# Splitting the first load of each batch, sharing the first products between two engines, and moving the softmax inside a pass

## The chip, the cores and the metric

The kernel runs on one core of one Trainium2 chip. The metric is device time in microseconds (us) for one execution. Ratios are computed as the mean time of one kernel's fast runs over that of the other's of the same rounds, so they are not quite the ratio of the medians quoted beside them. Different calls ran on different chips, and the kernel before took 1084 to 1090 us on them; differences of a few microseconds are therefore read from ratios, or from kernels of one call.

## The reference

Eight batches of 4096 tokens with 192 features. Each token gets a weighted sum of itself and the six tokens before it, with weights from a softmax over 7 per head; then two matrix products with `h - tanh(h)` between them.

```python
w = softmax(weight_gen, axis=-1)                  # [8, 4096, 8 heads, 7]
x_pad = concatenate([zeros(8, 6, 192), x], axis=1)
x = einsum('bshk,bskhg->bshg', w, windows_of_7(x_pad))   # -> [32768, 192]
h = x @ w_in                                      # [192, 2048]
out = (h - tanh(h)) @ w_out                       # [2048, 192]
```

## The kernel before

The work is cut into 32 passes of 1024 tokens, four to a batch. A pass `n` has eight steps, counted from 0. In each step TensorE makes two blocks of the first product for `n` (`gemm1`) and one block of the second for `n - 1` (`gemm2`); in steps 2 and 5 it also transposes and sums the seven weighted products for `n + 1` (`conv`). GpSimd makes those products (`products`), two passes ahead, and the softmax runs three passes ahead. The first tile of a batch has no tokens before its first row, so row 0 is loaded apart and its six missing tokens are cleared (`memzero`).

```python
    def load(n):
        ...
        lo = 0
        if s == 0:                                   # first pass of a batch
            lo = 1
            nc.vector.memzero(x_t[0:1, 0:HALO, :])
            nc.sync.dma_start(out=x_t[0:1, HALO : HALO + J, :], in_=x[b, 0:J]...)
        ...
        nc.sync.dma_start(out=x_t[lo:P, :, :], in_=src)     # 127 or 128 partitions

    def softmax(n):
        ...   # exp on ScalarE -> e_t; then on VectorE: zsum, zr = 1/zsum, wsm = e_t*zr

    def products(n):
        for k in range(K):
            nc.gpsimd.tensor_mul(prod_k, x_t[:, k : k + J, :]..., wsm[:, :, :, k : k + 1]...)
    ...
    for n in range(NTOT + 1):
        if n + 2 < NTOT:
            products(n + 2)
        if n + 3 < NTOT:
            load(n + 3)
        for p in range(J):
            ...  # gemm1 twice, gemm2; conv in steps 2 and 5
            if p == 5 and n + 3 < NTOT:
                softmax(n + 3)
```

The x tiles, the products and the output tiles have two buffers each. The blocks of the first product have three in PSUM.

The softmax here doesn't subtract the row's maximum and nothing guards it: scores larger than these inputs give would overflow.

Of the kernel before, what the change touches and what calls it, by code (L numbers as in the profile page):

```python
# [16 lines left out]
def kernel(  # L17
# [8 lines left out]
    nc = tc.nc  # L26

    B, S, D = x.shape
# [3 lines left out]
    P = nc.NUM_PARTITIONS  # L32
    R = P // 2
    HALO = K - 1

    J = 8
# [4 lines left out]
    NTOT = B * NSB  # L41
# [19 lines left out]

    x_of = {}
    wg_of = {}
    wsm_of = {}
    prods_of = {}
    conv_of = {}
# [3 lines left out]
    def load(n):  # L70
        b, s = divmod(n, NSB)
        s0 = s * TOK
        wg_t = wgpool.tile([P, J, H, K], FP32, name="wg_t")
        nc.sync.dma_start(
            out=wg_t[:],
            in_=weight_gen[b, s0 : s0 + TOK].rearrange("(p j) h k -> p j h k", p=P),
        )

        x_t = xpool.tile([P, HALO + J, D], FP32, name="x_t")
        lo = 0  # L80
        if s == 0:
            lo = 1
            nc.vector.memzero(x_t[0:1, 0:HALO, :])  # L83
            nc.sync.dma_start(out=x_t[0:1, HALO : HALO + J, :], in_=x[b, 0:J].rearrange("(p j) d -> p j d", p=1))
        win = x[b, s0 + lo * J - HALO : s0 + lo * J - HALO + 1]
        src = bass.AP(
            tensor=win.tensor,
            offset=win.offset,
            ap=[[J * D, P - lo], [D, HALO + J], [1, D]],
        )  # L90
        nc.sync.dma_start(out=x_t[lo:P, :, :], in_=src)
        wg_of[n] = wg_t
        x_of[n] = x_t

    def softmax(n):
        wg_t = wg_of.pop(n)
        e_t = wgpool.tile([P, J, H, K], FP32, name="e_t")
        nc.scalar.activation(  # L98
            out=e_t[:].rearrange("p j h k -> p (j h k)"),
            in_=wg_t[:].rearrange("p j h k -> p (j h k)"),  # L100
            func=ACT.Exp,
        )
        zsum = wgpool.tile([P, J * H], FP32, name="zsum")
        nc.vector.reduce_sum(  # L104
            out=zsum[:], in_=e_t[:].rearrange("p j h k -> p (j h) k"), axis=AX.X
        )
        zr = wgpool.tile([P, J * H], FP32, name="zr")
        nc.vector.reciprocal(zr[:], zsum[:])  # L108
        wsm = wgpool.tile([P, J, H, K], FP32, name="wsm")
        nc.vector.tensor_mul(  # L110
            wsm[:].rearrange("p j h k -> p (j h) k"),
            e_t[:].rearrange("p j h k -> p (j h) k"),
            zr[:].rearrange("p (n o) -> p n o", o=1).to_broadcast([P, J * H, K]),
        )
        wsm_of[n] = wsm

    def products(n):
        x_t = x_of.pop(n)
        wsm = wsm_of.pop(n)
        prods = []  # L120
        for k in range(K):

            prod = ppool.tile([P, NC, J, H, GC], BF16, name=f"prod{k}", tag=f"prod{k}")
            nc.gpsimd.tensor_mul(  # L124
                prod[:].rearrange("p c j h g -> p j h c g"),
                x_t[:, k : k + J, :].rearrange("p j (h c g) -> p j h c g", h=H, c=NC),
                wsm[:, :, :, k : k + 1]
                .rearrange("p j h (k o) -> p j h k o", o=1)
                .to_broadcast([P, J, H, NC, GC]),
            )  # L130
            prods.append(prod)
        prods_of[n] = prods

    def conv(n, chunks):

        prods = prods_of[n]
        if n not in conv_of:
            conv_of[n] = cpool.tile([P, NC, HT], BF16, name="convT")
        convT = conv_of[n]
        nch = len(chunks)  # L140
        pc = psum_h.tile([P, 2, HT], FP32, name="pc", tag="ph")
        for k in range(K):
            for ci, c in enumerate(chunks):
                for j in range(JH):
                    col = (ci * JH + j) * R
                    for r in range(2):
                        nc.tensor.matmul(  # L147
                            pc[:, r, col : col + R],
                            lhsT=prods[k][r * R : (r + 1) * R, c, 2 * j : 2 * j + 2].rearrange(
                                "p j h g -> p (j h g)"  # L150
                            ),
                            rhs=ident[r * R : (r + 1) * R, r * R : (r + 1) * R],
                            start=(k == 0 and ci == 0 and j == 0),
                            stop=(k == K - 1 and ci == nch - 1 and j == JH - 1),
                        )
        c0 = chunks[0]
        nc.scalar.activation(  # L157
            out=convT[:, c0 : c0 + nch, :].rearrange("p c (j r t) -> p r (c j) t", r=2, t=R),
            in_=pc[:, :, 0 : nch * JH * R].rearrange("p r (cj t) -> p r cj t", t=R),
            func=ACT.Copy,  # L160
        )
        if c0 + nch == NC:
            prods_of.pop(n)

    def gemm1(n, f):
        convT = conv_of[n]
        ph = psum_h.tile([P, 2, HT], FP32, name="ph", tag="ph")
        for c in range(NC):
            for r in range(2):
                nc.tensor.matmul(  # L170
                    ph[:, r, :],
                    lhsT=w_in[r * R : (r + 1) * R, c, f * P : (f + 1) * P],
                    rhs=convT[r * R : (r + 1) * R, c, :],
                    start=(c == 0),
                    stop=(c == NC - 1),
                )
        th = tpool.tile([P, TOK], FP32, name="th")
        ph_f = ph[:].rearrange("p r t -> p (r t)")
        last_act[0] = nc.scalar.activation(out=th[:], in_=ph_f, func=ACT.Tanh)  # L179
        gt = gpool.tile([P, TOK], BF16, name=f"gt{f}", tag=f"gt{f}")  # L180
        nc.vector.tensor_sub(gt[:], ph_f, th[:])  # L181
        g_of.setdefault(n, []).append(gt)
# [4 lines left out]
    def gemm2(i):  # L187
# [30 lines left out]
        if i > 0:  # L218
# [7 lines left out]
            if j == J - 1:  # L226
# [5 lines left out]
                )  # L232

    load(0)

    w_in = const.tile([P, NC, F], BF16, name="w_in")
    for r in range(2):
        for h in range(H):
            nc.gpsimd.dma_start(  # L239
                out=w_in[r * R + h * GC : r * R + (h + 1) * GC],  # L240
                in_=moe_w_in[h * G : (h + 1) * G].rearrange("(c g) f -> g c f", c=NC),
# [3 lines left out]

    ctx.enter_context(tc.manual_schedule())

    softmax(0)
    load(1)
    products(0)  # L250
    softmax(1)
    load(2)
    conv(0, (0, 1))
    conv(0, (2,))
    products(1)
    softmax(2)
    for n in range(NTOT + 1):
        if n + 2 < NTOT:
            products(n + 2)
# [3 lines that stand above are left out]
            if n < NTOT:  # L263
                gemm1(n, 2 * p)
                gemm1(n, 2 * p + 1)
            if n >= 1:
                gemm2((n - 1) * J + p)
            if n + 1 < NTOT:
                if p == 2:
                    conv(n + 1, (0, 1))  # L270
                if p == 5:
                    conv(n + 1, (2,))
            if p == 5 and n + 3 < NTOT:
                softmax(n + 3)
    gemm2(NTOT * J)


# [28 lines left out]
```

## Time and profile before

| | kernel before |
|---|---|
| median time | 1084.96 us (1082.41 to 1086.94, 4 runs) |
| span of the profiled run | 1082.9 us |
| busy: TensorE, VectorE, ScalarE, GpSimd | 74%, 62%, 59%, 60% |
| GpSimd waiting for x | 267.6 us in 8 waits |
| pass, undisturbed | 24.74 us |
| stop per batch | 23.2 us (worked out in the prediction; 23.6 once a misread start is corrected, see "Why the prediction was right") |

A line of a wait view reads: who waited, for what, total us, times, longest us. A timeline line reads: start, length, engine, line and operation, count, and in brackets how long the engine had been idle and what released it. The distance from one GpSimd set of seven products to the next is the length of a pass, a handy ruler. The lines themselves are in the prediction.

### The profile page before, as it was taken

Reading aid. Unit: us, or ns where it says so; the run is one execution under the profiler, and the core shown is the slowest. Engines: PE = TensorE matmul, PEld = TensorE weight load, DVE = VectorE, ACT = ScalarE, POOL = GpSimd, SP = SyncE. Lnnn points to the kernel's source line nnn. Section 1 sums busy time; section 2 is a strip of 40 time slices with the busy share of each in tenths; the row PEclk is TensorE's granted clock in tenths of the full one; section 3 lists DMA queues with packets and bytes.
Section 4 is the critical chain, followed back from the end, with each engine's and each line's share of the span. In section 5 each row is a group of like instructions: output and inputs, shape, how many; then the busy total and the mean of one; then the engine's idle time right before and its main releaser. Section 6 shows DMA issues by size and latency. Waiting matters only on the chain.

```text
span 1082.9 us, 36083 instructions
## 1 busy us (share of the span) xinstructions
PE 801.6 (74%) x16640; PEld 614.9 (57%) x16640; DVE 676.3 (62%) x616; ACT 642.6 (59%) x865; POOL 655.0 (60%) x247
## 2 busy tenths in 40 slices
PE   0004598689659993899749993899849993999996
PEld 0002276567446772777537772677637772777775
DVE  1003575588538882788628883788728883788782
ACT  0002465577437872687637882688627882787882
POOL 3029970999068771978259770978359770988200
PEclk9999799799869997999969997899969997999999
DMA  4501113141303222230402212130402212130001
GB/s 70 121 24 61 60 36 110 44 144 47 116 19 113 73 86 88 78 107 19 144 20 94 90 64 108 60 113 32 145 21 91 93 65 108 73 107 31 32 32 60
DMA packets 16952, 81.19 MB, mean 75 GB/s; under 512 B 4128, under 2 KB 8224, under 8 KB 12712
## 3 DMA queue, kind: packets, MB, share of 16 engines
q1 hardware_dynamic: 13712, 76.51, 19.7%
q0 software_dynamic: 3088, 2.36, 1.8%
q8 instruction: 130, 2.13, 0.8%
q14 instruction: 22, 0.18, 0.1%
HBM read 56.06 MB, written 25.17 MB: 75 GB/s over the span
## 4 chain that ended last, share of the span: by engine, by line
PE 47%; DMA 22%; DVE 10%; another core or an unknown queue 3%; issue 2%; ACT 2%; POOL 1%; DVEq 0%; ACTq 0%
PE po L200 22%; DMA out_dram<-out_sb 22%; PE ph L170 19%; PE pc L147 6%; DVE gt L181 5%; DVE wsm L110 3%; DVE zsum L104 1%; POOL prod L124 1%; ACT e_t L98 1%; DVE zr L108 1%; ACT out_sb L225 0%; ACT th L179 0%; ACT convT L157 0%; DVEq L110 0%
## 5 line engine op out<-in xcount | busy, mean ns | idle before, releaser
L124 POOL TENSOR_TENSOR prod<-x_t,wsm 128x1536 bf16<-128x1536 f32 x224 | 643.7, 2910 | 332.3 <-DMA x_t<-in_x_dram 267.6
L181 DVE TENSOR_TENSOR gt<-ph,th 128x1024 bf16<-128x1024 f32 x512 | 599.1, 1217 | 262.9 <-ACT th L179 259.9
L179 ACT ACTIVATE th<-ph 128x1024 f32<-128x1024 f32 x512 | 500.6, 1022 | 94.6 <-PE ph L170 93.6
L200 PE MATMUL po<-w_out,gt 64*128 64x192 bf16 x8192 | 398.5, 247 | 119.9 <-ACT out_sb L225 118.9
L200 PEld LDWEIGHTS <-gt 64*128 64x128 bf16 x8192 | 366.0, 96 | 175.5 <-issue 124.1
L170 PE MATMUL ph<-convT,w_in 64*128 64x512 bf16 x3072 | 404.6, 383 | 55.0 <-DVE gt L181 51.0
L170 PEld LDWEIGHTS <-w_in 64*128 64x128 bf16 x3072 | 167.4, 95 | 183.0 <-issue 92.9
L225 ACT ACTIVATE out_sb<-po 128x192 f32<-128x192 f32 x256 | 85.2, 333 | 166.4 <-DMA out_dram<-out_sb 120.6
L147 PE MATMUL pc<-ident,prod 64*128 64x64 bf16 x5376 | 99.5, 195 | 101.8 <-POOL prod L124 100.4
L147 PEld LDWEIGHTS <-prod 64*128 64x128 bf16 x5376 | 95.1, 98 | 104.7 <-POOL prod L124 102.0
L157 ACT ACTIVATE convT<-pc 128x1024 bf16<-128x1024 f32 x64 | 51.8, 810 | 91.2 <-PE pc L147 91.2
L104 DVE TENSOR_REDUCE zsum<-e_t 128x64 f32<-128x448 f32 x32 | 19.8, 620 | 116.5 <-ACT e_t L98 116.5
L98 ACT ACTIVATE e_t<-wg_t 128x448 f32<-128x448 f32 x32 | 18.2, 568 | 83.2 <-DMA wg_t<-in_weight_gen_dram 83.2
L110 DVE TENSOR_TENSOR wsm<-e_t,zr 128x448 f32<-128x448 f32 x32 | 34.4, 1076 | 2.7
L239 POOL DMA_DIRECT2D w_in<-in_moe_w_in_dram x16 | 9.4, 592 | 19.6 <-DMA w_in<-in_moe_w_in_dram 19.2
L108 DVE RECIPROCAL zr<-zsum 128x64 f32<-128x64 f32 x32 | 17.7, 553 | 1.1
L83 DVE MEMSET x_t<- 1x1152 uint32 x8 | 8.1, 1018 | 3.0 <-issue 1.1
L244 POOL DMA_DIRECT2D w_out<-in_moe_w_out_dram x1 | 1.2, 1203 | 1.9 <-DMA w_in<-in_moe_w_in_dram 1.9
L98 ACT ACT_TABLE_LOAD x1 | 1.3, 1283 | 0.7 <-PEq L290 0.7
masks.py:197 POOL MEMSET ident<- 128x128 bf16 x1 | 0.2, 205 | 0.3 <-POOLq L290 0.3
masks.py:199 POOL TENSOR_SCALAR_AFFINE_SELECT ident<-ident 128x128 bf16<-128x128 bf16 x1 | 0.3, 304 | 0.1
L290 POOL MEMSET const-float32-0.0<- 128x1 f32 x1 | 0.1, 98 | 0.2 <-issue 0.2
(3 smaller groups left out, 0.3 us busy)
## 6 DMA issues: line engine op xcount, KB each, us to landing
x_t<-in_x_dram SPq DMA_DIRECT2D x24, 1344.0 KB
out_dram<-out_sb SPq DMA_DIRECT2D x32, 768.0 KB
x_t<-in_x_dram SPq DMA_DIRECT2D x8, 1333.5 KB
wg_t<-in_weight_gen_dram SPq DMA_DIRECT2D x32, 224.0 KB
w_in<-in_moe_w_in_dram POOLq DMA_DIRECT2D x16, 96.0 KB, 19.0
w_out<-in_moe_w_out_dram POOLq DMA_DIRECT2D x1, 768.0 KB, 49.1
x_t<-in_x_dram SPq DMA_DIRECT2D x8, 6.0 KB
```

The lines of the kernel that those rows point to most:

```text
L98: nc.scalar.activation(out=e_t[:].rearrange("p j h k -> p (j h k)"), in_=wg_t[:].rearrange("p j h k -> p (j h k)"), func=ACT.Exp,)
L104: nc.vector.reduce_sum(out=zsum[:], in_=e_t[:].rearrange("p j h k -> p (j h) k"), axis=AX.X)
L108: nc.vector.reciprocal(zr[:], zsum[:])
L110: nc.vector.tensor_mul(wsm[:].rearrange("p j h k -> p (j h) k"), e_t[:].rearrange("p j h k -> p (j h) k"), zr[:].rearrange("p (n o) -> p n ...
L124: nc.gpsimd.tensor_mul(prod[:].rearrange("p c j h g -> p j h c g"), x_t[:, k : k + J, :].rearrange("p j (h c g) -> p j h c g", h=H, c=NC), ...
L147: nc.tensor.matmul(pc[:, r, col : col + R], lhsT=prods[k][r * R : (r + 1) * R, c, 2 * j : 2 * j + 2].rearrange("p j h g -> p (j h g)"), rh ...
L157: nc.scalar.activation(out=convT[:, c0 : c0 + nch, :].rearrange("p c (j r t) -> p r (c j) t", r=2, t=R), in_=pc[:, :, 0 : nch * JH * R].re ...
L170: nc.tensor.matmul(ph[:, r, :], lhsT=w_in[r * R : (r + 1) * R, c, f * P : (f + 1) * P], rhs=convT[r * R : (r + 1) * R, c, :], start=(c == ...
L179: last_act[0] = nc.scalar.activation(out=th[:], in_=ph_f, func=ACT.Tanh)
L181: nc.vector.tensor_sub(gt[:], ph_f, th[:])
L200: mm = nc.tensor.matmul(po[:, 0:D], lhsT=g_of[n][f][r * R : (r + 1) * R, col : col + P], rhs=w_out[r * R : (r + 1) * R, f, :], start=(r == ...
L225: last_act[0] = nc.scalar.activation(out=out_sb[:, j, :], in_=po[:, 0:D], func=ACT.Copy)
```

## The change

Its intent: speed up the first load of a batch, which takes 55 us for 1333.5 KB, shorten the way to the first matrix product, and take the softmax out of the way of TensorE.

```diff
@@ load
+        def rows(p0, p1):
+            ...                      # one x load of partitions p0 to p1
         if s == 0:
-            lo = 1
             nc.vector.memzero(x_t[0:1, 0:HALO, :])
             ...                      # row 0
+            rows(1, 16)
+            rows(16, P)
+        else:
+            rows(0, P)
@@ softmax -> softmax_exp (ScalarE) and softmax_norm (VectorE)
@@ products
+            eng = nc.vector if k in on_vector else nc.gpsimd
+            eng.tensor_mul(
@@ before the loop
-    products(0)
+    products(0, on_vector=(1, 3, 5, 6))
...
-    products(1)
+    products(1, on_vector=(2, 5))
@@ in the loop
+            if p == 1 and n + 3 < NTOT:
+                softmax_exp(n + 3)
             if n >= 1:
                 gemm2((n - 1) * J + p)
...
-            if p == 5 and n + 3 < NTOT:
-                softmax(n + 3)
+            if p == 2 and n + 3 < NTOT:
+                softmax_norm(n + 3)
```

More of the change, by code (lines that the diff above doesn't have):

```diff
@@ L63 @@
     wg_of = {}
+    e_of = {}
     wsm_of = {}
@@ L79, in load, with softmax_exp @@
         x_t = xpool.tile([P, HALO + J, D], FP32, name="x_t")
-        lo = 0
+        def rows(p0, p1):
+            win = x[b, s0 + p0 * J - HALO : s0 + p0 * J - HALO + 1]
+            nc.sync.dma_start(
+                out=x_t[p0:p1, :, :],
+                in_=bass.AP(
+                    tensor=win.tensor,
+                    offset=win.offset,
+                    ap=[[J * D, p1 - p0], [D, HALO + J], [1, D]],
+                ),
+            )
         if s == 0:
-            lo = 1
             nc.vector.memzero(x_t[0:1, 0:HALO, :])
-            nc.sync.dma_start(out=x_t[0:1, HALO : HALO + J, :], in_=x[b, 0:J].rearrange("(p j) d -> p j d", p=1))
-        win = x[b, s0 + lo * J - HALO : s0 + lo * J - HALO + 1]
-        src = bass.AP(
-            tensor=win.tensor,
-            offset=win.offset,
-            ap=[[J * D, P - lo], [D, HALO + J], [1, D]],
-        )
-        nc.sync.dma_start(out=x_t[lo:P, :, :], in_=src)
+            nc.sync.dma_start(
+                out=x_t[0:1, HALO : HALO + J, :],
+                in_=x[b, 0:J].rearrange("(p j) d -> p j d", p=1),
+            )
+            rows(1, 16)
+            rows(16, P)
+        else:
+            rows(0, P)
         wg_of[n] = wg_t
         x_of[n] = x_t
-    def softmax(n):
+    def softmax_exp(n):
         wg_t = wg_of.pop(n)
@@ L102, in softmax, with softmax_norm @@
         )
+        e_of[n] = e_t
+    def softmax_norm(n):
+        e_t = e_of.pop(n)
         zsum = wgpool.tile([P, J * H], FP32, name="zsum")
@@ L115, in softmax, with products @@
         wsm_of[n] = wsm
-    def products(n):
+    def products(n, on_vector=()):
         x_t = x_of.pop(n)
@@ L123, in products @@
             prod = ppool.tile([P, NC, J, H, GC], BF16, name=f"prod{k}", tag=f"prod{k}")
-            nc.gpsimd.tensor_mul(
+            eng = nc.vector if k in on_vector else nc.gpsimd
+            eng.tensor_mul(
                 prod[:].rearrange("p c j h g -> p j h c g"),
@@ L246 @@
     ctx.enter_context(tc.manual_schedule())
-    softmax(0)
+    softmax_exp(0)
+    softmax_norm(0)
     load(1)
-    products(0)
-    softmax(1)
+    products(0, on_vector=(1, 3, 5, 6))
+    softmax_exp(1)
+    softmax_norm(1)
     load(2)
@@ L254 @@
     conv(0, (2,))
-    products(1)
-    softmax(2)
+    products(1, on_vector=(2, 5))
+    softmax_exp(2)
+    softmax_norm(2)
     for n in range(NTOT + 1):
```

## The prediction

> **What bounds the kernel now.** I read the page's busy shares first, then the waits by total, then the chain of work that ended last between 360 and 460 us, then the timelines of the SyncE queue, TensorE, GpSimd and VectorE around one of its long pieces.
>
> Busy shares and waits:
>
> ```profile
> PE 801.6 (74%) x16640; PEld 614.9 (57%) x16640; DVE 676.3 (62%) x616; ACT 642.6 (59%) x865; POOL 655.0 (60%) x247
> ...
> POOL prod L124 <- DMA x_t<-in_x_dram: 267.6, 8, 41.2
> ...
> ACT out_sb L225 <- DMA out_dram<-out_sb: 120.6, 6, 23.5
> PE po L200 <- ACT out_sb L225: 118.9, 15, 22.6
> ```
>
> No engine is above 74%: something stops all of them together. GpSimd waits 8 times for x, once for each of the 8 batches (a batch is four passes of 1024 tokens). ScalarE waits 6 times for an output store to finish, and TensorE then waits for ScalarE. The queue and the chain show one of these (start, length):
>
> ```profile
> 374.05 0.25 SPq L91 DMA_DIRECT2D x_t<-in_x_dram  x1
> 384.62 11.77 SPq L229 DMA_DIRECT2D out_dram<-out_sb  x1
> ...
> 384.62 46.36 DMA out_dram<-out_sb
> ...
> 431.45 2.74 PE L200 MATMUL po<-w_out,gt 64*128 64x192 bf16 x32 [18.20 <-ACT out_sb L225]
> ...
> 429.27 20.06 POOL L124 TENSOR_TENSOR prod<-x_t,wsm 128x1536 bf16<-128x1536 f32 x7 [30.80 <-DMA x_t<-in_x_dram]
> ```
>
> The batch's first x load leaves at 374.05 and GpSimd can start on it at 429.27: 55 us for 1333.5 KB, some 25 GB/s. The store that left after it lands at 431, although a store is only 768 KB. TensorE stops for 18.2 us, and its next 32 matmuls take 2.74 us instead of the usual 1.32 us.
>
> Between such stops the kernel is bound by TensorE. GpSimd starts a set of seven products every 24.74 us (599.08 to 623.82, and 843.56 to 868.29), and in one such stretch (columns: PE, PEld, DVE, ACT, POOL busy, then granted clock, DMA share, GB/s):
>
> ```profile
> 843.50:868.30 24.80, 23.96 (x524) 18.55 (x521) 20.52 (x20) 20.06 (x28) 20.07 (x8) 1.00 0.16 52
> ```
>
> TensorE is busy for 23.96 of 24.80 us at full clock. The largest hole in it is 0.75 us, behind the softmax:
>
> ```profile
> 869.35 0.82 PE L170 MATMUL ph<-convT,w_in 64*128 64x512 bf16 x6 [0.75 <-DVE gt L181]
> ```
>
> [...] wsm takes 0.62 us when GpSimd is idle and up to 3.33 us beside the products, while the reduction, with one input, stays at 0.62 us.
>
> **The change, part by part.**
>
> Split load, at the 7 later batches. 1 + 15 + 112 partitions: [...] What each stop costs is read from where passes start. Pass 1 begins its first matmuls at about 132.8 us and pass 31 at 1037.4: 904.6 us for 30 passes. Thirty undisturbed ones take 30 x 24.74 = 742.2, so 162.4 us, or 23.2 per batch, is the stops. I expect all of it to go.
>
> Start. Now GpSimd begins its products at 74.64, because the first x load takes from 1.55 to there. [...] So after the change I estimate x in place at 8 to 10 us, GpSimd free of its DMA issue at 17 (33.4 now), and w_in there at 25 to 28. VectorE makes products 1, 3, 5 and 6: 1536 elements by the rate of wsm (448 elements in 0.62 us, about 0.15 of it fixed) is 1.75 us each, 7 us, done before GpSimd starts. GpSimd's three take 3 x 2.87 = 8.6: at 25 to 26. The first set thus ends near 26 instead of 95. [...] The third, 20.06 us on GpSimd alone: 63. Pass 0 is short (no second matmul) and ends near 58, but pass 1 needs the third set, also because VectorE's clearing of the x tile of batch 1 waits for it. So pass 1 starts effectively at 62 instead of 132.8: 71 us gained. Of this the load is most; the shared products are worth about 10 us, by 20.06 - 8.6 in the first set and 2 in the second.
>
> Softmax apart. The same instructions run: one exp (0.57) and 0.62 + 0.55 + 0.62 on VectorE. Exp goes to step 1 of 8 of a pass and the normalisation to step 2, beside 1.63 us of transposing matmuls that need no VectorE, where it stood at step 5 beside 0.83. VectorE also saves its 0.47 us wait for exp. By itself that would close most of the 0.75 us hole. But now the products start right after wsm, so wsm always meets an idle GpSimd in undisturbed passes. With the normalisation early they will start once step 5 has freed their buffers, and run about 20 us, to some 13 us into the next pass. Step 2's wsm, some 9 us in, falls among them and waits up to 2.87 us. The place is nearly fixed: from the end of step 5 to wsm is about 16.5 to 17 us, and a product boundary lies at 6 x 2.87 = 17.2. So I expect a wait near 0.5 us, with 2.9 possible if it just misses. A pass without any hole would take 24.74 - 0.75 = 24.0; I take 24.4.
>
> Sum: 62 + 30 x 24.4 + 2 (seven clearings, about 0.3 each) + the last 45.5 (1037.4 to 1082.9, unchanged) = 841.5. Launch times lie a microsecond above the span: 842 us.
>
> **The rivals.** (a) *The normalisation collides with the products.* With a full 2.87 us wait in each pass, a pass takes up to 26.5 and the kernel 905. For it: the 3.33 us wsm now. Against: three PSUM buffers and the 1.63 us of transposes absorb part, and the geometry favours a short wait. (b) *Start bound by the weights.* If the w_in loads keep their pace of 2.3 us whatever x does, GpSimd is free at 33.4, w_in lands at 50, pass 1 starts near 76: 856. [...] (c) *The store wait remains*, [...]: at half of today's stops, 81 us more, 923. Against: with 128-partition loads now the queue issues in 0.33 us and no store wait appears. (d) *TensorE throttled when it no longer rests.* Against: granted clock 1.00 throughout 930 to 1080 us. [...]
>
> **Range and chances.** Pass length 24.0 to 25.2 gives 830 to 866 with the start at 62; a start of 55 to 76 moves it by -7 to +14. These partly offset: 822 to 868. Every part of the big sum would have to fail for a gain under 2% (22 us), as the start alone is worth 71: faster 0.985, same 0.01, slower 0.005.
>
> **What would show it.** Right: no wait of the products for x beyond the start; the store waits under 5 us in all; the first product before 20 us, on VectorE at about 1.75 us; pass 1 starting near 62; sets of products 24.0 to 25 us apart; granted clock near 1.00 after the start. Wrong: passes above 25.5 us with wsm near 3 us (rival a); GpSimd's first product after 30 us (rival b); a long store at batch starts (rival c). My weakest number is the pass length, since every 0.1 us in it is 3 us of the total.

The sum came to 841.5 us, 842 with the launch. The start was built like this: GpSimd free of its issue at 17 us, its three products to 26, the second set of 17.9 us to 43, the third of 20.06 us to 63, and from these pass 1 effectively at 62. The 8 to 10, the 17 and the 25 to 28 us there rested on estimates; so did the time in which the split load should land, 3.4 us. What the trace of the kernel before shows of its long load: from 416 to 427 us, while it and one output store were under way, the mean busy share of the core's 16 DMA engines was 0.06, at 26 GB/s.

## The result, and the profile after

The changed kernel takes 861.48 us (median of 4 runs, 859.23 to 864.49), a ratio of 0.7943 to the kernel before, 95% interval 0.7911 to 0.7975.

The page of the changed kernel, its span and its busy line:

```profile
span 860.7 us, 36095 instructions
...
PE 779.2 (91%) x16640; PEld 604.4 (70%) x16640; DVE 707.5 (82%) x622; ACT 641.3 (75%) x865; POOL 644.9 (75%) x241
```

TensorE now works for 91% of the time. The engines have no less to do (GpSimd handed six products to VectorE, some 10 us on either): the time came out of standing still. Waits by total, changed kernel:

```profile
POOL prod L141 <- PE pc L164: 121.7, 28, 8.3
...
ACT out_sb L242 <- PE po L217: 36.2, 73, 1.9
...
DVE prod L141 <- DMA x_t<-in_x_dram: 9.5, 2, 8.5
...
PE po L217 <- ACT out_sb L242: 3.8, 9, 0.4
```

GpSimd no longer waits for x at all; it waits for TensorE to free product buffers, as an engine with time to spare should. ScalarE's wait for output stores is gone, and TensorE's wait for ScalarE fell from 118.9 us to 3.8. The two large pieces of the split load, from the page's list of transfers (KB each, then median us from issue to landing):

```profile
x_t<-in_x_dram SPq DMA_DIRECT2D x8, 1176.0 KB, 7.0
...
x_t<-in_x_dram SPq DMA_DIRECT2D x8, 157.5 KB, 3.2
```

7.0 us in place of some 55. While the pieces of one such load were under way, with logits beside them (72.6 to 79.7 us), the mean busy share of the 16 DMA engines was 0.85, at 220 GB/s, against the 0.06 and 26 GB/s of the long load. Now two stretches of the changed kernel, an ordinary pass and one in which a batch's first tile is cleared (columns as in the prediction: length, then busy us of PE, PEld, DVE, ACT, POOL, clock, DMA share, GB/s):

```profile
120.50:144.30 23.80, 23.69 (x532) 18.53 (x524) 20.83 (x20) 19.88 (x28) 20.45 (x7) 1.00 0.29 102
...
467.00:494.00 27.00, 24.34 (x554) 18.76 (x548) 24.07 (x22) 20.43 (x28) 20.19 (x8) 1.00 0.38 125
```

In the ordinary one TensorE is idle for 0.11 us of 23.80. In the other it is idle for 2.66. The ruler, GpSimd's timeline of the changed kernel, shows both kinds:

```profile
144.33 20.45 POOL L141 TENSOR_TENSOR prod<-x_t,wsm 128x1536 bf16<-128x1536 f32 x7 [3.38 <-PE pc L164]
168.16 20.06 POOL L141 TENSOR_TENSOR prod<-x_t,wsm 128x1536 bf16<-128x1536 f32 x7 [3.38 <-PE pc L164]
196.56 20.45 POOL L141 TENSOR_TENSOR prod<-x_t,wsm 128x1536 bf16<-128x1536 f32 x7 [8.34 <-PE pc L164]
```

23.83 us, then 28.40. Six such long distances stand in the trace: 28.40, 28.33, 26.75, 26.74, 26.74 and 28.40. What happens in one of them, on VectorE and TensorE, below the normalisation of an ordinary pass (436.11):

```profile
436.11 1.04 DVE L126 TENSOR_TENSOR wsm<-e_t,zr 128x448 f32<-128x448 f32 x1
...
474.88 1.02 DVE L94 MEMSET x_t<- 1x1152 uint32 x1 [0.18 <-PE po L217]
...
484.42 3.25 DVE L126 TENSOR_TENSOR wsm<-e_t,zr 128x448 f32<-128x448 f32 x1
...
488.86 0.82 PE L187 MATMUL ph<-convT,w_in 64*128 64x512 bf16 x6 [2.04 <-DVE gt L198]
```

The clearing makes VectorE late, wsm takes 3.25 us instead of 1.04, the subtraction behind it is late, and TensorE stands for 2.04 us. The products' rhythm shows how narrow the miss is: in that pass a product began at 484.29 us, 0.13 us before wsm was due, and wsm ended 0.48 us after that product's end at 487.19; in the ordinary pass it was due 0.56 us before a product's end (436.67), and ended 0.48 us after it too. The first of the seven later clearings (76.87 us) meets no collision: wsm takes 0.83 us there.

In three of the six passes TensorE also ran at half speed for a while after a hole of 2.17 us (granted clock 0.50 from 190.7 to 194.0, 289.8 to 293.0 and 685.7 to 688.9 us; the next 32 small matmuls took 2.49 to 2.81 us instead of 1.50), which makes the 28.4 out of 26.7:

```profile
189.88 0.82 PE L187 MATMUL ph<-convT,w_in 64*128 64x512 bf16 x6 [2.17 <-DVE gt L198]
190.53 2.65 PE L217 MATMUL po<-w_out,gt 64*128 64x192 bf16 x32
```

Last, the start of the changed kernel, on GpSimd, VectorE and TensorE:

```profile
27.13 1.20 POOL L261 DMA_DIRECT2D w_out<-in_moe_w_out_dram  x1 [1.27 <-DMA w_in<-in_moe_w_in_dram]
28.35 22.92 POOL L141 TENSOR_TENSOR prod<-x_t,wsm 128x1536 bf16<-128x1536 f32 x8
...
14.62 6.76 DVE L141 TENSOR_TENSOR prod<-x_t,wsm 128x1536 bf16<-128x1536 f32 x4 [8.52 <-DMA x_t<-in_x_dram]
...
42.44 9.32 DVE L126 TENSOR_TENSOR wsm<-e_t,zr 128x448 f32<-128x448 f32 x1
...
52.95 4.02 PE L187 MATMUL ph<-convT,w_in 64*128 64x512 bf16 x18 [10.54 <-DVE gt L198]
```

VectorE has made its four products by 21.4 us. GpSimd is busy with issuing weight loads until 28.3. Then a third wsm, needed only much later, stands in VectorE's queue for 9.32 us, until GpSimd's row of eight products ends, and the first subtractions wait behind it.

### The profile page after: what moved, and what is told of

Same layout as the page of the kernel before. It is cut to its first block, busy times and chain, and to the rows that moved or that the text cites. A ratio compares the mean times of both kernels' runs of the same rounds, so it can differ in the third digit from the quotient of the medians.

```text
span 860.7 us, 36095 instructions
## 1 busy us (share of the span) xinstructions
PE 779.2 (91%) x16640; PEld 604.4 (70%) x16640; DVE 707.5 (82%) x622; ACT 641.3 (75%) x865; POOL 644.9 (75%) x241
## 3 DMA queue, kind: packets, MB, share of 16 engines
q0 software_dynamic: 3088, 2.36, 2.1%
q8 instruction: 130, 2.13, 1.0%
## 4 chain that ended last, share of the span: by engine, by line
PE 66%; DVE 21%; ACT 7%; issue 2%; DMA 2%; POOL 2%; DVEq 0%; POOLq 0%
PE po L217 31%; PE ph L187 31%; DVE gt L198 15%; ACT th L196 6%; PE pc L164 4%; DVE wsm L126 4%; DMA w_in<-in_moe_w_in_dram 2%; POOL prod L141 1%; DVE zr L124 1%; DVE zsum L120 1%; POOL w_in L256 1%; ACT out_sb L242 1%; DVE x_t L94 0%; ACT e_t L110 0%; POOL ident masks.py:199 0%
## 5 line engine op out<-in xcount | busy, mean ns | idle before, releaser
L141 POOL TENSOR_TENSOR prod<-x_t,wsm 128x1536 bf16<-128x1536 f32 x218 | 633.6, 2943 | 122.4 <-PE pc L164 121.7
L187 PE MATMUL ph<-convT,w_in 64*128 64x512 bf16 x3072 | 397.1, 381 | 35.4 <-DVE gt L198 31.7
L217 PEld LDWEIGHTS <-gt 64*128 64x128 bf16 x8192 | 359.2, 95 | 57.7 <-issue 5.7
L217 PE MATMUL po<-w_out,gt 64*128 64x192 bf16 x8192 | 390.6, 244 | 4.8 <-ACT out_sb L242 3.8
L187 PEld LDWEIGHTS <-w_in 64*128 64x128 bf16 x3072 | 169.3, 95 | 155.6 <-issue 63.2
L164 PE MATMUL pc<-ident,prod 64*128 64x64 bf16 x5376 | 93.7, 192 | 36.8 <-POOL prod L141 35.0
L164 PEld LDWEIGHTS <-prod 64*128 64x128 bf16 x5376 | 89.8, 96 | 38.2 <-POOL prod L141 35.3
L126 DVE TENSOR_TENSOR wsm<-e_t,zr 128x448 f32<-128x448 f32 x32 | 56.2, 1756 | 2.7
L120 DVE TENSOR_REDUCE zsum<-e_t 128x64 f32<-128x448 f32 x32 | 19.5, 609 | 15.7 <-ACT e_t L110 15.7
L141 DVE TENSOR_TENSOR prod<-x_t,wsm 128x1536 bf16<-128x1536 f32 x6 | 10.2, 1754 | 9.5 <-DMA x_t<-in_x_dram 9.5
```

The lines of the kernel that those rows point to most:

```text
L120: nc.vector.reduce_sum(out=zsum[:], in_=e_t[:].rearrange("p j h k -> p (j h) k"), axis=AX.X)
L126: nc.vector.tensor_mul(wsm[:].rearrange("p j h k -> p (j h) k"), e_t[:].rearrange("p j h k -> p (j h) k"), zr[:].rearrange("p (n o) -> p n ...
L141: eng.tensor_mul(prod[:].rearrange("p c j h g -> p j h c g"), x_t[:, k : k + J, :].rearrange("p j (h c g) -> p j h c g", h=H, c=NC), wsm[: ...
L164: nc.tensor.matmul(pc[:, r, col : col + R], lhsT=prods[k][r * R : (r + 1) * R, c, 2 * j : 2 * j + 2].rearrange("p j h g -> p (j h g)"), rh ...
L187: nc.tensor.matmul(ph[:, r, :], lhsT=w_in[r * R : (r + 1) * R, c, f * P : (f + 1) * P], rhs=convT[r * R : (r + 1) * R, c, :], start=(c == ...
L217: mm = nc.tensor.matmul(po[:, 0:D], lhsT=g_of[n][f][r * R : (r + 1) * R, col : col + P], rhs=w_out[r * R : (r + 1) * R, f, :], start=(r == ...
```

## The experiments

Three questions: which part gave what, what makes the clearing passes long, and what bounds the start. My theory of the long passes was that the 1.02 us clearing shifts the normalisation so that it just misses a product boundary on GpSimd. The rivals were the transfers of a batch's start, and the clearing's own time.

### Each part alone and left out

**The split load alone** is the kernel before with only the change in `load`.

> The kernel before with the split x load alone. My theory: the seven stops vanish (no store wait over 5 us), passes stay at the 24.74 us that undisturbed passes of the kernel before show, and GpSimd alone makes the first sets of products (20 us each from about 28 us on), so pass 1 starts near 88 us: 88 + 30 x 24.74 + 2 + 45.5 = 878 us. Rival, that the stops were not the load but the order of the queue: stores still wait, over 940 us. Rival, that the vector engine's products are of no use at the start: pass 1 starts at 75 us as in the changed kernel, 865 us.

882.51 us, ratio 0.8105 (0.8075 to 0.8134). The seven stops are gone with this part alone, and passes are 24.74 us, as expected. A batch's first products (the middle line) no longer wait for x, and TensorE's wait for ScalarE is as short as in the changed kernel:

```profile
190.89 20.06 POOL L141 TENSOR_TENSOR prod<-x_t,wsm 128x1536 bf16<-128x1536 f32 x7 [4.67 <-PE po L217]
216.09 20.06 POOL L141 TENSOR_TENSOR prod<-x_t,wsm 128x1536 bf16<-128x1536 f32 x7 [5.13 <-PE po L217]
240.74 20.07 POOL L141 TENSOR_TENSOR prod<-x_t,wsm 128x1536 bf16<-128x1536 f32 x7 [4.59 <-PE po L217]
...
PE po L217 <- ACT out_sb L242: 3.8, 9, 0.4
```

The run is 4.5 us longer than the sum. Pass 1 starts near 92 us rather than 88, and five sets between 315 and 442 us lie 25.2 to 25.4 us apart, clearing or not, which nothing in the trace that I looked at explains.

**Without the split softmax**: exp and normalisation together again at step 5.

```diff
-            if p == 1 and n + 3 < NTOT:
-                softmax_exp(n + 3)
-            if p == 2 and n + 3 < NTOT:
-                softmax_norm(n + 3)
+            if p == 5 and n + 3 < NTOT:
+                softmax_exp(n + 3)
+                softmax_norm(n + 3)
```

> The changed kernel with exp and normalisation together again at step 5. My theory: pass 1 starts at 75 us as in the changed kernel, passes are 24.74 us with a 0.75 us hole, and batch passes are only about 0.3 us longer, since normalisation meets an idle GpSimd: 75 + 742 + 2 + 45.5 = 864.5 us. So the split softmax is worth only some 3 us in the changed kernel (0.9 us in each pass, most of it given back in the seven passes that clear). Rival, that the split softmax is worth its 0.9 us in all 30 passes: this kernel 888 us.

863.39 us, ratio 0.7955 (0.7916 to 0.7994). The changed kernel's 0.7943 lies within that interval, so the split softmax has no clear worth here. GpSimd's timeline of this run shows why: both kinds of pass differ from the changed kernel's, in opposite directions.

```profile
543.83 20.07 POOL L141 TENSOR_TENSOR prod<-x_t,wsm 128x1536 bf16<-128x1536 f32 x7 [4.67 <-PE po L217]
568.57 20.06 POOL L141 TENSOR_TENSOR prod<-x_t,wsm 128x1536 bf16<-128x1536 f32 x7 [4.68 <-PE po L217]
593.76 20.07 POOL L141 TENSOR_TENSOR prod<-x_t,wsm 128x1536 bf16<-128x1536 f32 x7 [5.13 <-PE po L217]
```

An ordinary pass takes 24.74 us (0.91 more), a clearing pass 25.19 (1.6 to 3.2 less). Per batch the split softmax gains 3 x 0.91 = 2.7 us and loses 1.6 to 3.2.

**Without the shared products**: the changed kernel with `on_vector` left out.

> The changed kernel with all products on GpSimd. My theory: the first set takes 20 us instead of 8.6 and the second 20 instead of 14.4, so pass 1 starts some 13 us later than in the changed kernel: 861.5 + 13 = 874.5 us, passes as there (23.83, and 26.7 to 28.4 in the clearing ones). Rival, that the vector engine's products [...] delay the weights: then without them GpSimd is free of its issue at about 20 us instead of 28.3, and the total is near 866 us.

875.57 us, ratio 0.8055 (0.8027 to 0.8083): my number within 1.1 us. The sharing is worth 14 us here (12 by the ratios; in the traces pass 1 begins at 88.27 us instead of 74.48), and 882.51 - 863.39 = 19 us where the softmax is together. The rival falls: GpSimd issues w_out at 27.12 us here too, so VectorE's products do not hold up the weights.

**The split softmax alone**, on the kernel before.

> The kernel before with exp and normalisation apart as in the changed kernel, and nothing else. The stops stay. Theory: each stop ends [...] 55 us after the load's issue, so what passes save while that load runs is lost in a longer stop; only the other 67 us of a batch's 122 count, some 2.7 passes x 0.9 us, less what the clearing gives back: 1085 - 7 x 2 = 1071 us or up to 1085. Rival, that savings add up whatever the stops do: 30 x 0.9 less, 1058 us.

1065.0 us, ratio 0.9777 (0.9753 to 0.9801). A miss: it saves 24.7 us against the kernel before of the same call, more than my 14 and nearly what the rival said. It is a saving of about 2%, small but clear of the noise. The structure of my reason holds, its size does not. A batch still has one stop, released some 56 us after its load's issue. One batch starts its first products at 783.21 us, issues the next long load at 845.34 and can use it at 901.37. From the first products to that issue it takes 62.1 us; in the kernel before, the same stretch (798.14 to 863.93) takes 65.8. So the saving lies ahead of the issue, and is 3.7 us there instead of the 2 that I gave it. Over the last five batches the period falls from 122.1 to 118.0 us. What waits has changed, as the waits of this run show: exp waits for the logits. In the batch looked at they were issued at 869.47 us, after the long load of 845.34, and exp could begin at 903.53, after a wait of 15.47 us.

```profile
ACT e_t L99 <- DMA wg_t<-in_weight_gen_dram: 193.7, 9, 71.8
```

### What makes the clearing passes long

**Clearing later**: the seven later clearings are emitted after the normalisation, in step 3.

```diff
-            nc.vector.memzero(x_t[0:1, 0:HALO, :])
+            if n == 0:
+                nc.vector.memzero(x_t[0:1, 0:HALO, :])
...
+            if p == 3 and n + 3 < NTOT and (n + 3) % NSB == 0:
+                nc.vector.memzero(x_of[n + 3][0:1, 0:HALO, :])
```

> The changed kernel with the 1.02 us clearing of the batch's first x tile emitted after step 3 instead of at the start of a pass (seven of them). My theory: at the start of the pass it shifts the normalisation so that its last instruction just misses a boundary of the GpSimd products and waits for a whole one (3.25 us instead of 1.04), which opens a hole of 2.0 us in TensorE and in some passes a spell at half clock. Moved, all passes take 23.8 us and wsm stays near 1 us: 861.5 - 22 = 839 us. Rival, that batch passes are long because of their transfers (split load, stores): they stay at 26.7 us or more, 860 us.

847.99 us, ratio 0.7796 (0.7777 to 0.7816): 13.5 us better than the changed kernel by the medians (16 by the ratios), not 22. The rival falls, as the transfers are the same; but the clearing is not free in step 3 either. GpSimd's timeline:

```profile
460.95 20.45 POOL L142 TENSOR_TENSOR prod<-x_t,wsm 128x1536 bf16<-128x1536 f32 x7 [3.38 <-PE pc L165]
485.63 20.45 POOL L142 TENSOR_TENSOR prod<-x_t,wsm 128x1536 bf16<-128x1536 f32 x7 [4.23 <-PE pc L165]
```

24.68 us, 0.85 more than an ordinary pass: VectorE has 20.8 us of work in 23.8, and 1.02 us more right behind the normalisation still makes it late (TensorE then stands for 0.62 us, waiting for a subtraction). One of the seven passes took 27.54 us (361.75 to 389.29). In it TensorE stood for 1.44 us and its transposes later came 0.48 us late, both put down to "issue", that is, to nothing that the profile shows; after that wsm took 2.10 us, before this pass's clearing. So a small shift lengthens wsm without a clearing too, though here it is only a part of the loss.

**wsm on GpSimd**: the third instruction of the normalisation moves to the engine that it collides with, and the clearing stays at the start of the pass.

```diff
-        nc.vector.tensor_mul(
+        (nc.gpsimd if on_gpsimd else nc.vector).tensor_mul(     # False for the first two
             wsm[:].rearrange("p j h k -> p (j h) k"),
```

> The changed kernel with the last instruction of the normalisation (wsm) on GpSimd itself, from the third set of products on; the clearing stays where it is. My theory: the long clearing passes come from the collision of wsm with the products, not from the 1.02 us of clearing. GpSimd cannot collide with itself and has 3.4 us to spare in a pass, so clearing passes fall from 26.7 to about 24.4 us (the 0.55 us hole behind the clearing stays), other passes stay at 23.83, and the vector engine is not held for 9.3 us at the start: 861.5 - 7 x 2.7 - 4 = 838.5 us. Rival, that the clearing itself costs the time: clearing passes stay at 26.7 us, 858 us.

841.61 us, ratio 0.7732 (0.7707 to 0.7756). GpSimd's timeline, from one clearing pass:

```profile
163.88 20.07 POOL L141 TENSOR_TENSOR prod<-x_t,wsm 128x1536 bf16<-128x1536 f32 x7 [2.81 <-issue]
183.90 0.98 POOL L126 TENSOR_TENSOR wsm<-e_t,zr 128x448 f32<-128x448 f32 x1
188.41 20.07 POOL L141 TENSOR_TENSOR prod<-x_t,wsm 128x1536 bf16<-128x1536 f32 x7 [3.54 <-issue]
```

The clearing pass is 24.53 us long with the clearing where it was. This separates the two: of the 2.9 us that a clearing costs at full clock, about 0.7 is the clearing and the rest the collision. (Moving wsm also takes about 1 us of work off VectorE in every pass. That relief alone is not the cause: in the run before, VectorE kept that work and a clearing cost 0.85 us.) At the start, VectorE's 9.3 us were gone (first subtraction at 41.25 us instead of 51.68), and pass 1 began at 63.03 us instead of 74.48. But then the clearing for the second batch waited until GpSimd had finished its third set:

```profile
71.27 1.02 DVE L94 MEMSET x_t<- 1x1152 uint32 x1 [6.04 <-POOL prod L141]
```

Pass 1 took 35.27 us instead of 28.04, so pass 2 began at 98.30 us instead of 102.53: 4.2 us of the 11.4 were kept, about the 4 that I expected. At the start GpSimd's chain of products was the next bound behind wsm.

### What bounds the start

**The second x load behind the weights**: its issue moves to GpSimd's queue, after w_out.

```diff
-            rows(0, P)
+            rows(0, P, nc.gpsimd if n == 1 else nc.sync)
```

> The changed kernel with the second block's x load issued by GpSimd behind all weight loads, so that it cannot share the transfer engines with them. Theory: what keeps GpSimd issuing until 27 us is that x and weight rows share all 16 engines (their busy share is 0.83 to 1.08 from 0 to 30 us); 1344 KB less beside them gives w_out's issue at about 21 us, first products on GpSimd at about 22 to 23 instead of 28.3, and the whole 4 to 6 us less: 856 us. Rival, that the weight loads have a pace of their own (they convert to bf16): w_out's issue stays near 27 us and the kernel is as fast or slower, 861 to 866 us.

859.64 us, ratio 0.7892 (0.7868 to 0.7915), about 2 us better than the changed kernel; the intervals touch. The first number of the theory, w_out's issue at about 21 us, holds:

```profile
21.58 1.21 POOL L261 DMA_DIRECT2D w_out<-in_moe_w_out_dram  x1
...
34.58 4.48 POOL L141 TENSOR_TENSOR prod<-x_t,wsm 128x1536 bf16<-128x1536 f32 x1 [2.56 <-DMA x_t<-in_x_dram]
```

w_out is issued at 21.58 us instead of 27.13, as expected. But the second set of products then waits for its x until 34.58, and the clearing for the second batch for GpSimd's third set (until 73.10 us). The gain is passed on to the next wait: pass 1 begins 8.7 us earlier than in the changed kernel, pass 2 only 2.2.

**All of it together**: wsm and the later clearings on GpSimd, the first set of products wholly on VectorE.

```diff
-            nc.vector.memzero(x_t[0:1, 0:HALO, :])
+            (nc.gpsimd if n else nc.vector).memzero(x_t[0:1, 0:HALO, :])
...
-    products(0, on_vector=(1, 3, 5, 6))
+    products(0, on_vector=range(K))
```

> As the run before in this list, with the later clearings on GpSimd too and the first set of products wholly on the vector engine, which waits for nothing there while GpSimd issues the weights. My theory: all passes 23.83 us (7 x 0.6 us less), and GpSimd starts the second set at 28 us instead of 37, so pass 1 starts some 7 us earlier: 838.5 - 4 - 7 = 828 us. If the start is bound by the weights' landing instead, 834 us.

824.31 us, ratio 0.757 (0.7548 to 0.7592), better than both kernels and 4 us better than expected. GpSimd's timeline around a clearing, and TensorE at the start:

```profile
533.82 20.07 POOL L141 TENSOR_TENSOR prod<-x_t,wsm 128x1536 bf16<-128x1536 f32 x7 [2.82 <-issue]
553.83 1.05 POOL L94 MEMSET x_t<- 1x1152 uint32 x1
554.85 0.96 POOL L126 TENSOR_TENSOR wsm<-e_t,zr 128x448 f32<-128x448 f32 x1
557.64 20.07 POOL L141 TENSOR_TENSOR prod<-x_t,wsm 128x1536 bf16<-128x1536 f32 x7 [1.84 <-issue]
...
30.12 4.00 PE L187 MATMUL ph<-convT,w_in 64*128 64x512 bf16 x17 [1.95 <-DMA w_in<-in_moe_w_in_dram]
```

The pass with a clearing takes 23.82 us like the others. The first product of the matrices begins at 27.56 us, and after one matmul it waits until 30.12 for the landing of w_in, for the first time. Pass 2 begins at 85.34 us, 13.0 earlier than with wsm alone moved; the clearings give the other 4 of the 17 us between these two runs. TensorE is busy for 711 of the 716 us between 84 and 800.

## Why the prediction was right, and where its terms were off

The time lay in the range (842 predicted, 822 to 868, measured 861.5), 19 us above the middle. Its steps:

**The stops vanish, worth 162 us: right.** The split load alone removes them (no store wait is left), and it carries most of the change: a ratio of 0.8105 where the whole reaches 0.7943. With it alone, the 30 passes from 1 to 31 take 157.6 us less than before. One reading was off by a step: pass 31 begins at 1039.99 us, not at 1037.4, where the last step of pass 30 begins. So the stops were worth 165 us, and the end of the kernel takes 42.9 us, not 45.5. (The usual 32 matmuls, too, take 1.50 us on the timeline, not 1.32.) The load was put at 3.4 us to landing, by an estimate whose basis no run showed, and took 7.0, which cost nothing that the trace shows, as no product waits for x after the start.

**Start, 62 us: 12 us too early.** Pass 1 begins its first matrix product near 74.5 us. Three terms of the sum failed. "x in place at 8 to 10 us" measured 14.6, when VectorE's first product could begin; as VectorE was still done by 21.4, this cost nothing. "GpSimd free of its DMA issue at 17" measured 28.3. I had estimated that the weights' pace would fall to near 1 us per w_in load, which no run had shown. From the ninth w_in load to w_out it was 2.13 us in the changed kernel (10.06 to 27.13 us) and 2.35 in the kernel before (13.39 to 32.21). In the changed kernel the mean busy share of the 16 DMA engines was 0.83, 1.08 and 0.85 in the first three stretches of 10 us, and the second x load and the logits, which leave at 2.4 to 4.6 us, were under way too; with only the second x load moved away the issue ended at 22.8. And VectorE's 9.32 us wait in wsm was not in the sum; with wsm moved away, pass 2 began 4.2 us earlier. One term was too long, which hid part of this: the second set took 14.3 us on GpSimd, not 17.9, because VectorE had made its two products before. "1.75 us each" for VectorE's products was exact (1.754); the 0.15 us of fixed time in it, an estimate, also follows from wsm (448 elements in 0.62 us) and the subtraction (1024 elements in 1.217 us), if both take the same time per element. "The shared products are worth about 10 us" measured 12 to 14.

**A pass, 24.4 us: right for ordinary passes in kind, 0.6 too long.** They take 23.83, and wsm 1.04 us: the predicted wait of about 0.5 us is there (0.42 over the 0.62 of an idle GpSimd), but opens no hole.

**Seven clearings, "about 0.3 each": the step that failed worst.** The six that can be read off the ruler cost 2.9 to 4.6 us each, 22.4 in all. I had named the danger ("2.9 possible if it just misses") and the cause of a miss stood in my own list of parts, but I counted the clearing as time and not as a shift. With wsm on GpSimd a clearing costs 0.7 us, so the collision is shown as the larger part; the spells at half speed come on top in half of the cases.

**The sum**: pass 31 of the changed kernel begins at 817.80 us, so its 30 passes take 743.3 us against the 734 predicted (732 and 2 for the clearings), and the end takes 42.9 us, as before. That is 12.5 us too little at the start, 9.3 too little in the passes and 2.6 too much at the end, together 19.2 of the 19.5 us. That the passes came so near is partly luck: the ordinary pass was 0.57 us too long, 17.1 us in 30 passes, and this hid most of the 26.4 us that clearings and small disturbances took beyond the 2 foreseen.

**The rivals**: (a), the collision, came true in one pass of four. (b), the late start, came true in size (I had 76 us for pass 1) but not for the reason given: the issue of the weights does depend on x, as it ended at 22.8 us instead of 28.3 with the second x load moved away. (c) and (d) did not come; the granted clock was 0.984 over the span against 0.924.

## What to carry to other kernels

Compare the landing times of loads of similar size, and look for stores that land late beside a slow one. Here a load of 127 partitions took 55 us for 1333.5 KB, and a store of 768 KB issued after it 46.4 us; cut into row 0 and pieces of 15 and 112 partitions, the two pieces landed in 3.2 and 7.0 us, and stores in 3.8. Where an instruction takes longer beside another engine's (wsm: 0.62 us with GpSimd idle, 3.25 beside the products), moving it by a microsecond can cost a wait of a foreign instruction's length, so ask of every added piece what it shifts, not only how long it is; moving the colliding instruction onto the other engine removed the question (0.97 us there, and a clearing cost 0.7 us instead of 2.9). A start is a chain of several near-equal bounds, and taking away the first one shows the second.

## What the traces showed besides

- wsm beside the products: in the two passes read above it ended 0.48 us after the end of the product that ran when it was due (1.04 and 3.25 us, products 2.87 us apart). At the start it waited through several products: 9.32 us in the changed kernel, and 15.89 us in the run with the split load alone, each time until 0.5 us after the end of GpSimd's row. When VectorE gets in between two instructions, no run here settles.
- GpSimd against VectorE: 1.65 times the time for a product (2.90 against 1.75 us for 1536 elements) and 1.56 times for wsm (0.97 against 0.62 us for 448).
- TensorE at half speed: in the changed kernel it followed holes of 2.17 us in three passes. A fourth hole of 2.17 us, and those of 2.04 and 1.34 us, were not followed by it. Why is not shown, and no run was made to test it.
- The weight loads: in the first 40 us of the changed kernel these transfers, which convert to bf16, took 46.0% of the 16 DMA engines' time for 2.36 MB, and the others 43.4% for 4.03 MB. That the conversion is the cause is not shown: their packets are also smaller, 3088 of them for those 2.36 MB against 791 for the 4.03.
